# A word of the entry tile cleared behind every sixth list scatter, and 28 row steps instead of 3 ahead of expert 0's last products

## The chip, the core and the metric

One core of a Trainium2 chip runs the whole program. TensorE (PE) multiplies, VectorE (DVE), ScalarE (ACT) and GpSimd (POOL) do the elementwise work, SyncE (SP) issues most transfers; the indirect transfers, which gather and scatter rows by a list of indices, are issued by POOL. The metric is the device time of one execution in microseconds (us); lower is better.

## What is computed

Attention over 32 memory slots for 8 batches of 576 tokens and 8 heads gives a matrix x of 4608 rows by 512. A mixture of experts follows, of which the reference says:

```
noisy_logits = logits + noise_scale * noise
top2 = np.argpartition(-noisy_logits, 2, axis=1)[:, :2]
...
for e in range(E):            # 8 experts
    for k in range(2):
        mask = top2[:, k] == e
        h = np.maximum(x[mask] @ w1[e], 0.0)          # 512 -> 1024
        out[mask] += top2_w[mask, k, None] * (h @ w2[e])   # 1024 -> 512
```

Every token goes to two of eight experts, so each expert has a list of about 1150 tokens.

## The kernel before

**Routing.** The tokens are worked off in four pairs of batches, P = 0 to 3, each of 9 tiles of 128 tokens. `gate` finds the two experts of each token, builds in the tile `ent` one 16-word entry for each of a token's two choices (the first two words hold the row number and the weight, the others are zero), and sends 18 indirect scatters (L570), one for each tile and choice, which put the entries into the experts' lists in memory. Three `ent` tiles are used in turn. Scatters are declared independent of each other, except that in the first three pairs every sixth one waits for the scatter issued before it (`hold`). POOL issues the scatters, and between them the products `vb` (L341) of the attention.

**Rows of an expert.** An expert's rows, at most 1216, come in two halves of five tiles (expert 0: four groups, 0 to 3). For experts 1 to 7 `gather_sums` fetches a half in three row tiles (128, 128 and 64 rows or, in the second half, 32). For each row tile two gathers on POOL (L793) bring `gsum` and `gtile`; DVE forms sums and differences in place (L810, L811, L825, L826); ACT writes their upper half precision part and DVE the rest, in three splits: `ghalf<-gsum`, `ghalf<-gtile`, `gsplit<-gsum` (L820, L821); each split is followed by a transposing transfer on SP's queue into the tile `xt` (L822). For expert 0 `gather` does the same without sums (L757, L768, L771, L772). The gathered tiles, the splits and `xt` live in rings of two or three buffers, so a step may have to wait until an earlier transfer has read its buffer.

**Products of an expert.** `mm1` (expert 0, L935) and `mm1_sums` (experts 1 to 7, seven products of sums for each of four column blocks, L851) multiply `xt` by w1; the result is cut into `hh` and `hl` by ACT and DVE (expert 0: copy `r` L941, `hh` L942, `hl` L943). `mm2` (L965) multiplies these by w2, ACT scales the result into `y` (L977), and POOL adds it to the output by an indirect transfer (L995). Expert 0 keeps its partial results in a ring of three PSUM banks, `mp`. The weights of an expert are loaded into `stg` (L604), squared and summed on ACT for a scale (L644), and split into `wh` and `wl` (ACT L654, DVE L657).

**What sets the order.** The attention and the first three groups of expert 0 are put in order by a table of times. Behind that the code's own order counts: each engine's instructions get priorities in the order in which the code emits them, and a scheduler places them by these and by what they wait for. `all_rows` is one long generator over all halves, of which each step emits one gather or one piece of a split; `step_side` advances it, and the weights' generator, by one step between the pieces of the products. A step that must not come too early yields "wait". Ahead of the loop over halves the code runs:

```
    allr = all_rows()
    ...
    pq[1] = prep(1)
    w_load(1, 0)
    run(allr, 3)
    run(pq[1], 4)
    side += [allr, pq[1]]
```

The first 8 steps of `allr` belong to expert 0's last group (0, 3), the following ones to expert 1's first half (1, 0). Before the products of a half, `need` runs `allr` on until that half is complete.

Of the kernel before, what the change touches and what calls it, by code (L numbers as in the profile page):

```python
# [20 lines left out]
NP = B // 2  # L21
# [4 lines left out]
LW = 16  # L26
# [25 lines left out]
BURST = 6  # L52
# [9 lines left out]
def tile_attn_moe(ctx, tc, q_t, phi_t, kv, wgn, noise, w1, w2, out):  # L62
    nc = tc.nc
    V, A, G, T = nc.vector, nc.scalar, nc.gpsimd, nc.tensor
# [415 lines left out]
    scatters, reads, gated = [], [], set()  # L480
    ents_used = []

    def gate(P, j0, j1):
        nj = j1 - j0
        ns = ns_all[:, P, j0:j1]
        lg = LG[P][:, j0:j1]
        isb = ISB[P][:, j0:j1]

        def t(name):
            return gs.tile([128, NJ, E], F32, name=name)[:, 0:nj]  # L490

        def t1(name):
            return gs.tile([128, NJ], F32, name=name)[:, 0:nj]

        def wide(x):
            return x[:, :, None].to_broadcast([128, nj, E])


        u, ln, r, d = t("gu"), t("gln"), t("gr"), t("gk")
        V.tensor_tensor(lg, lg, isb[:, :, None].to_broadcast([128, nj, 16]), OP.mult)  # L500
        A.activation(u, lg[:, :, 8:16], AF.Exp)
        V.tensor_scalar(r, u, 1.0, None, op0=OP.add)
        A.activation(ln, r, AF.Ln)
        V.tensor_scalar(d, r, 1.0, None, op0=OP.subtract)
        V.scalar_tensor_tensor(r, d, 0.0, d, op0=OP.is_equal, op1=OP.add)
        V.reciprocal(r, r)
        V.tensor_tensor(r, u, r, OP.mult)
        V.tensor_tensor(r, r, ns, OP.mult)
        V.scalar_tensor_tensor(ln, d, 0.0, ln, op0=OP.is_equal, op1=OP.add)
        V.tensor_tensor(ln, ln, r, OP.mult)  # L510
        nl = t("gnl")
        V.tensor_tensor(nl, ln, lg[:, :, 0:8], OP.add)
        ms, ks = [], []
        for i in range(2):
            m = t1("gm%d" % i)
            V.tensor_reduce(m, nl, axis=AX.X, op=OP.max)
            c = t("gr")
            V.tensor_tensor(c, nl, wide(m), OP.is_lt)
            V.scalar_tensor_tensor(c, c, 8.0, iota_e[:, 0:nj], op0=OP.mult, op1=OP.add)
            ix = t1("gi")  # L520
            V.tensor_reduce(ix, c, axis=AX.X, op=OP.min)
            k = t("gk%d" % i)
            V.tensor_tensor(k, iota_e[:, 0:nj], wide(ix), OP.is_equal)
            if i == 0:
                V.scalar_tensor_tensor(nl, k, -3.0e38, nl, op0=OP.mult, op1=OP.add)
            ms.append(m)
            ks.append(k)
        mb = gs.tile([128, NJ, E], BF16, name="gmb")[:, 0:nj]
        V.tensor_tensor(mb, ks[0], ks[1], OP.add)
        yield  # L530

        mbf = mb.rearrange("p j e -> p (j e)")
        pp = ptr.tile([128, 512], F32, name="tr")
        po = pp[:, 0:nj * E]
        T.matmul(po, tri, mbf, start=True, stop=False)
        for k in range(1, nj):
            T.matmul(po[:, k * E:], ones_bf, mbf[:, 0:(nj - k) * E], start=False, stop=(k == nj - 1))
        pc = pp[:, NJ * E:(NJ + 1) * E]
        for k in range(nj):
            T.matmul(pc, ones_bf, mbf[:, k * E:(k + 1) * E], start=(k == 0), stop=(k == nj - 1))  # L540
        n = 256 * sum(x < P for x in NEED)
        if j0 == 0 and n:
            V.tensor_scalar(base[:, 0:1], base[:, 0:1], float(n), None, op0=OP.max)
        ad = t("gk")
        V.tensor_tensor(ad, eoff[:, 0:nj], base[:, None, :].to_broadcast([128, nj, E]), OP.add)
        V.tensor_tensor(ad, ad, po.rearrange("p (j e) -> p j e", e=E), OP.add)
        V.tensor_tensor(base, base, pc, OP.add)
        idx = gs.tile([128, NJ, 2], I32, name="gidx", bufs=3)
        ent = ents[len(ents_used) % 3]
        ents_used.append(0)  # L550
        G.iota(ent[:, 0:nj, :, 0].bitcast(I32), pattern=[[128, nj], [0, 2]],
               base=TRASH + P * TP + j0 * 128, channel_multiplier=1)
        ai = gs.tile([128, 2, NJ], F32, name="gai")[:, :, 0:nj]
        for k in range(2):
            tt = t(("gu", "gln")[k])
            V.tensor_tensor(tt, ad, ks[k], OP.mult)
            V.tensor_reduce(ai[:, k, :], tt, axis=AX.X, op=OP.add)
        V.tensor_copy(idx[:, 0:nj].rearrange("p j k -> p k j"), ai)
        ex, den = t1("gex"), t1("gden")
        V.tensor_tensor(ex, ms[1], ms[0], OP.subtract)  # L560
        A.activation(ex, ex, AF.Exp)
        V.tensor_scalar(den, ex, 1.0, 1e-9, op0=OP.add, op1=OP.add)
        V.reciprocal(den, den)
        V.tensor_tensor(ex, ex, isb, OP.mult)
        V.tensor_tensor(ent[:, 0:nj, 0, 1], isb, den, OP.mult)
        V.tensor_tensor(ent[:, 0:nj, 1, 1], ex, den, OP.mult)
        yield
        for j in range(nj):
            for k in range(2):
                sc = G.indirect_dma_start(  # L570
                    out=lst[:, :], out_offset=bass.IndirectOffsetOnAxis(ap=idx[:, j, k:k + 1], axis=0),
                    in_=ent[:, j, k, :], in_offset=None)
                hold = P < NP - 1 and (2 * (j0 + j) + k) % BURST == 0
                for _, o in scatters[:-1] if hold else scatters:
                    tc.declare_no_dep(sc.ins, o.ins, reason="distinct list slots")
                scatters.append((P, sc))
                for p, o in reads:
                    if p < P:
                        tc.declare_no_dep(sc.ins, o.ins, reason="slots of earlier pairs")
                if (j0 + j, k) == (NJ - 1, 1):  # L580
                    gated.add(P)
                yield
# [16 lines left out]
    def w_load(e, i):  # L599
        WS[e, i] = {}  # L600
        loaded[e, i] = ticks[0]
        for c in (3, 0, 1, 2) if e == 1 and i == 0 else (0, 2, 1, 3) if e else range(4):
            s = WS[e, i][c] = mpool.tile([128, 1024], F32, name="stg%d" % c)
            d = nc.sync.dma_start(s, (w1, w2)[i][e, c])  # L604
            if e == 0:
                after(d, "kv", BUF["w2" if i else "w1"] + c * BUF["ws"])
# [396 lines left out]
    def run(it, n=10 ** 9):  # L1003
        for _ in range(n):
            x = next(it, "end")
            if x == "end":
                return
            ticks[0] += x == "wait"
# [104 lines left out]
    def routing(P, j0, j1, end):  # L1113
        t = max(end + max(0.0, PRI["gate"]), gate_at[-1])
        g = gate(P, j0, j1)
        add(t, run, g, 1)
        t = add(t + max(0.0, PRI["g2"]), run, g, 1)
        gate_at.append(add_low(t + max(0.0, PRI["gs"]), PRI["sc%d" % P], run, g))
# [50 lines left out]
    def all_rows():  # L1169
        for k, x in enumerate(seq):  # L1170
            yield from rows_in(k, *x)
            ready.add(x)
    allr = all_rows()
# [3 lines left out]
            run(it, 1)  # L1177
    pq[1] = prep(1)
    w_load(1, 0)
    run(allr, 3)  # L1180
    run(pq[1], 4)
    side += [allr, pq[1]]
    for k, (e, g) in enumerate(seq):
# [78 lines left out]
```

## Time and profile before

| | us |
|---|---|
| median of 3 runs | 1004.69 (1001.67 to 1005.63) |
| the profiled execution | 1002.9 |
| its span, first to last instruction | 1000.9 |
| PE busy in the span | 918.5 (92%) |
| DVE, ACT, POOL busy | 616.2, 579.4, 337.2 |
| longest single wait of PE from 200 us on | 13.72 |

All times of the trace are counted from the span's start. The program's parts follow each other on PE: attention with expert 0's first groups up to about 260 us, expert 0's last group from 261.6 to 300.8, then experts 1 to 7, some 94 us each.

### The profile page before, as it was taken

To read this page: it belongs to the slowest core of one execution; us is meant where nothing else is said; L and a number is where in the kernel's file an instruction comes from. 1 tells how busy PE (TensorE), PEld (TensorE's weight loads), DVE (VectorE), ACT (ScalarE), POOL (GpSimd) and SP (SyncE) were. 2 spreads that over 40 slices of the span, in tenths; PEclk is the share of its full clock that TensorE was granted. 3 is DMA by queue.
4 is the path that set the end of the run, shared out by engine and by line. 5 is a ranking of instruction groups with operands and counts; after the bars stand their busy time and mean duration, and the time that the engine had idled before them with its cause. 6 is when DMAs were issued, how large, how long until landed. Compare 5 with 4: busy or idle time off the path is not lost.

```text
span 1000.9 us, 17556 instructions
## 1 busy us (share of the span) xinstructions
PE 918.5 (92%) x6440; PEld 540.0 (54%) x6440; DVE 616.2 (62%) x1407; ACT 579.4 (58%) x1187; POOL 337.2 (34%) x307
## 2 busy tenths in 40 slices
PE   3898996989894999999999999999999999999995
PEld 2465654655342555465555656564646564656552
DVE  1547788642662858575866776576849585957140
ACT  3577775532542756656665767576757666765241
POOL 3122654774222142414141514232333323240303
PEclk9999997999997999999999999999999999999997
DMA  9999979937687778776786869586947794775403
GB/s 319 316 308 324 352 268 344 224 83 119 121 140 98 161 120 162 149 146 99 180 151 116 132 147 179 98 163 120 204 85 148 141 213 74 158 123 82 63 1 48
DMA packets 197910, 162.01 MB, mean 162 GB/s; under 512 B 152064, under 2 KB 162496, under 8 KB 195776
## 3 DMA queue, kind: packets, MB, share of 16 engines
q1 hardware_dynamic: 178144, 120.43, 49.2%
q0 software_dynamic: 19680, 40.45, 23.9%
q8 instruction: 51, 0.84, 0.4%
q14 instruction: 35, 0.29, 0.1%
HBM read 86.77 MB, written 41.07 MB: 128 GB/s over the span
## 4 chain that ended last, share of the span: by engine, by line
PE 66%; DMA 10%; DVE 9%; ACT 4%; issue 4%; POOL 2%; SPq 2%; POOLq 0%; ACTq 0%; DVEq 0%
PE ps L965 18%; PE mp L965 15%; PE ps L851 13%; PE mp L851 7%; DMA xt<-ghalf 4%; PE pb L851 3%; PE mp L935 3%; SPq L703 2%; DMA stg<-in_w 1%; PE xp L470 1%; PE xp L355 1%; DMA phs<-in_phi_t 1%; PE tr L435 1%; PE tr L315 1%; DVE wl L657 1%
## 5 line engine op out<-in xcount | busy, mean ns | idle before, releaser
L995 POOL DMA_INDIRECT out<-y,lt x80 | 137.3, 1716 | 269.3 <-ACT y L977 239.1
L965 PEld LDWEIGHTS <-hh 128*128 128x128 f16 (+2 forms) x1504 | 122.3, 99 | 145.2 <-issue 15.9
L851 PE MATMUL ps<-xt,wh 128*128 128x320 f16 (+1 forms) x560 | 140.1, 295 | 17.6 <-DMA xt<-ghalf 15.1
L965 PE MATMUL ps<-wh,hl 128*128 128x512 f16 (+2 forms) x400 | 125.4, 380 | 0.0
L965 PE MATMUL ps<-wl,hh 128*128 128x512 f16 (+2 forms) x400 | 124.9, 380 | 0.0
L965 PE MATMUL ps<-wh,hh 128*128 128x512 f16 (+2 forms) x400 | 121.5, 380 | 0.0
L851 PEld LDWEIGHTS <-wh 128*128 128x128 f16 x896 | 87.0, 98 | 54.7 <-DMA xt<-ghalf 16.1
L965 PE MATMUL mp<-wh,hh 128*128 128x512 f16 (+2 forms) x352 | 113.0, 380 | 3.5 <-ACT hh L864 1.3
L965 PE MATMUL mp<-wl,hh 128*128 128x512 f16 (+2 forms) x352 | 113.0, 380 | 0.0
L965 PE MATMUL mp<-wh,hl 128*128 128x512 f16 (+2 forms) x352 | 112.0, 380 | 0.8 <-DVE hl L865 0.8
L965 PEld LDWEIGHTS <-hl 128*128 128x128 f16 (+2 forms) x752 | 63.1, 99 | 72.5 <-issue 6.9
L851 PE MATMUL ps<-xt,whx 128*128 128x320 f16 (+1 forms) x336 | 96.3, 292 | 0.0
L793 POOL DMA_INDIRECT gtile<-xs,lt x28 | 32.2, 1151 | 186.8 <-DVE ghalf L821 148.6
L654 ACT ACTIVATE wh<-stg,wsc 128x512 f16<-128x512 f32 x112 | 76.1, 713 | 30.8 <-DVE wsc L381 19.6
L570 POOL DMA_INDIRECT lst<-gent,gidx x72 | 72.1, 1002 | 37.0 <-issue 20.0
L657 DVE SCALAR_TENSOR_TENSOR wl<-stg,wsc,wh 128x1024 f16<-128x1024 f32 (+1 forms) x63 | 73.0, 1161 | 14.9 <-ACT wh L654 14.5
L851 PEld LDWEIGHTS <-whx 128*128 128x128 f16 x672 | 65.8, 98 | 28.0 <-issue 3.8
L644 ACT ACTIVATE wl<-stg 128x1024 bf16<-128x1024 f32 x56 | 58.6, 1047 | 28.9 <-DMA stg<-in_w 22.2
L851 PE MATMUL ps<-xt,wl 128*128 128x320 f16 (+1 forms) x280 | 73.7, 295 | 0.0
L857 ACT ACTIVATE r<-ps 128x320 f32<-128x320 f32 (+1 forms) x112 | 46.8, 421 | 39.7 <-PE ps L851 26.4
L793 POOL DMA_INDIRECT gsum<-xs,lt x42 | 48.1, 1144 | 63.1 <-DVE gsplit L821 52.8
L851 PE MATMUL mp<-xt,wh 128*128 128x320 f16 (+1 forms) x224 | 64.8, 292 | 0.9 <-DMA xt<-ghalf 0.7
(214 smaller groups left out, 1852.8 us busy)
## 6 DMA issues: line engine op xcount, KB each, us to landing
stg<-in_w SPq DMA_DIRECT2D x64, 512.0 KB
kvs<-in_kv SPq DMA_DIRECT2D x16, 1024.0 KB
out<-zt SPq DMA_DIRECT2D x38, 256.0 KB
qs<-in_q_t SPq DMA_DIRECT2D x16, 576.0 KB
xs<-xr SPq DMA_DIRECT2D x36, 256.0 KB
phs<-in_phi_t SPq DMA_DIRECT2D x16, 288.0 KB
kvs<-in_kv SPq DMA_DIRECT2D x16, 128.0 KB
xt<-ghalf SPq DMA_TRANSPOSE x88
```

Of the source, the lines that this page charges most:

```text
L315: mark["kv", u] = T.matmul(pk[h * 32:(h + 1) * 32, 0, :], es[:K, c, h * 32:(h + 1) * 32], kvs[:K, c, h, :], start=(c == 0), stop=(c == 4))
L570: sc = G.indirect_dma_start(out=lst[:, :], out_offset=bass.IndirectOffsetOnAxis(ap=idx[:, j, k:k + 1], axis=0), in_=ent[:, j, k, :], in_of ...
L644: (id if first else pace)(A.activation(wl[:, c * 1024:c * 1024 + 1024].bitcast(BF16), s[c], AF.Square, accum_out=am[:, c:c + 1]))
L654: (id if first else pace)(A.activation(h[:, o + k:o + k + 512], x[:, k:k + 512], AF.Identity, scale=sc))
L657: V.scalar_tensor_tensor(l[:, o:o + n], x, sc, h[:, o:o + n], op0=OP.mult, op1=OP.subtract)
L703: d = nc.sync.dma_start(dst, src)
L793: G.indirect_dma_start(out=x[:n], out_offset=None, in_=xs[:, :], in_offset=bass.IndirectOffsetOnAxis(ap=ix.bitcast(I32), axis=0))
L851: mark["pe"] = T.matmul(ps[:, :nh], t[w][:, o:o + 128], xt[:, 4 * k0 + 2 * n0 * lo + 2 * (a - k0) + c, :nh], start=(first and m == 0), sto ...
L857: A.activation(y[:, :nh], ps[:, :nh], AF.Identity, scale=SHC)
L935: d = mark["pe"] = mark["mm1", g] = T.matmul(ps[:, :n], ww[:, c * FF + f * 128:c * FF + (f + 1) * 128], xt[:, xo + c, :n], start=(k == 0), ...
L965: mark["pe"] = T.matmul(ps[lo:lo + x.shape[-1]], x, ws, start=start, stop=stop)
L995: d = G.indirect_dma_start(out=out[:, :], out_offset=bass.IndirectOffsetOnAxis(ap=LT[e][:n, t, 0:1].bitcast(I32), axis=0), in_=y[:n], in_o ...
```

## The change

Every sixth scatter of the first three pairs no longer waits for the one before it. Instead POOL clears the last word (which is zero already) of the entry that the sixth and the twelfth scatter of a pair read; such a write has to wait until that scatter's transfer has read the entry. These are six writes of 128 x 1 in the whole program. And `allr` is run 28 steps, not 3, before expert 1's weights and expert 0's last products are emitted.

```
-                hold = P < NP - 1 and (2 * (j0 + j) + k) % BURST == 0
-                for _, o in scatters[:-1] if hold else scatters:
+                for _, o in scatters:
                     tc.declare_no_dep(sc.ins, o.ins, reason="distinct list slots")
                 scatters.append((P, sc))
                 for p, o in reads:
                     if p < P:
                         tc.declare_no_dep(sc.ins, o.ins, reason="slots of earlier pairs")
+                if (2 * j + k) % BURST == BURST - 1 and (j, k) != (nj - 1, 1) and P < NP - 1:
+                    G.memset(ent[:, j, k, LW - 1:LW], 0.0)
...
     pq[1] = prep(1)
     w_load(1, 0)
-    run(allr, 3)
+    run(allr, 28)
     run(pq[1], 4)
```

In the changed program lines from 579 on stand one later (L820 is L821).

On DVE, in the products of expert 0's group 2 (`hh`, `hl` of 256 columns), there stood before:

```order
L771 TENSOR_TENSOR ghalf<-gtile,ghalf 128x512 x2
L942 CAST hh<-r 128x256
L943 TENSOR_TENSOR hl<-r,hh 128x256
L942 CAST hh<-r 128x256
L943 TENSOR_TENSOR hl<-r,hh 128x256
L942 CAST hh<-r 128x256
```

and now there stands:

```order
L772 TENSOR_TENSOR ghalf<-gtile,ghalf 128x512 x2
L943 CAST hh<-r 128x256
L944 TENSOR_TENSOR hl<-r,hh 128x256
L943 CAST hh<-r 128x256
L811 TENSOR_TENSOR gsum<-gtile 128x256
L944 TENSOR_TENSOR hl<-r,hh 128x256
L812 TENSOR_TENSOR gtile<-gsum,gtile 128x256
```

The two row sums of expert 1's first row tile have moved between the second `hh` and its `hl`.

On ACT, from the last square of expert 1's w1 (`wl,wam<-stg`) to the first copy `r` of expert 0's last group (448 columns), there stood before:

```order
L644 ACTIVATE wl_3546,wam<-stg_3534 128x1024
L977 ACTIVATE y<-mp,wlu 128x512
L654 ACTIVATE wh_3545<-stg_3530,wsc 128x512
L654 ACTIVATE wh_3545<-stg_3534,wsc 128x512 x2
L654 ACTIVATE wh_3545<-stg_3532,wsc 128x512
L654 ACTIVATE whx<-stg_3528,wsc 128x512 x2
L941 ACTIVATE r<-mp 128x448
```

and now there stands:

```order
L645 ACTIVATE wl_3597,wam<-stg_3540 128x1024
L821 ACTIVATE ghalf<-gsum 128x512
L821 ACTIVATE ghalf<-gtile 128x512
L978 ACTIVATE y<-mp,wlu 128x512
L821 ACTIVATE gsplit<-gsum 128x768
L655 ACTIVATE wh_3596<-stg_3536,wsc 128x512
L655 ACTIVATE wh_3596<-stg_3540,wsc 128x512 x2
L655 ACTIVATE wh_3596<-stg_3538,wsc 128x512
L655 ACTIVATE whx<-stg_3534,wsc 128x512 x2
L942 ACTIVATE r<-mp 128x448
```

The three splits of expert 1's first row tile have moved ahead of the weights' splits and of `r`; they stood among and behind them.

Also on ACT, at the end of expert 0's last group (`y` of its tiles), there stood before:

```order
L941 ACTIVATE r<-mp 128x448 x2
L977 ACTIVATE y<-mp,wlu 128x512
L977 ACTIVATE y<-ps_3820,wlu 128x512
L820 ACTIVATE ghalf<-gtile 128x512
L644 ACTIVATE wl_3810,wam<-stg_3801 128x1024
L820 ACTIVATE gsplit<-gsum 128x768
L644 ACTIVATE wl_3810,wam<-stg_3803 128x1024
L820 ACTIVATE ghalf<-gsum 64x512
L977 ACTIVATE y<-mp,wlu 128x512
L820 ACTIVATE ghalf<-gtile 64x512
```

and now there stands:

```order
L942 ACTIVATE r<-mp 128x448 x3
L821 ACTIVATE ghalf<-gsum 64x512
L821 ACTIVATE gsplit<-gsum 64x768
L978 ACTIVATE y<-mp,wlu 128x512
L821 ACTIVATE ghalf<-gtile 64x512
L978 ACTIVATE y<-ps_3848,wlu 128x512
L645 ACTIVATE wl_3826,wam<-stg_3817 128x1024
L645 ACTIVATE wl_3826,wam<-stg_3819 128x1024
L645 ACTIVATE wl_3826,wam<-stg_3821 128x1024
L645 ACTIVATE wl_3826,wam<-stg_3823 128x1024
```

The second row tile's splits are no longer in this stretch, and two of the third row tile's three (64 rows) have moved ahead of the first `y`; all four squares of expert 1's w2 stand behind it. PE's own order hardly changes there: pieces of expert 0's last `mm2` move by one column block.

## Rows read from the trace of the kernel before

**Rows 1.** the page, part 1: busy us (share of span) xinstructions by engine
```profile
PE 918.5 (92%) x6440; PEld 540.0 (54%) x6440; DVE 616.2 (62%) x1407; ACT 579.4 (58%) x1187; POOL 337.2 (34%) x307
```
**Rows 2.** waits of PE, whole span: us in total, times, longest
```profile
PE ps L851 <- DMA xt<-ghalf: 15.1, 2, 13.7
PE mp L935 <- DMA xt<-ghalf: 3.3, 1, 3.3
```
**Rows 3.** windows: length, busy us by engine, granted clock, DMA share, GB/s
```profile
262.00:301.00 39.00, 38.79 (x199) 17.93 (x197) 27.72 (x51) 19.06 (x34) 10.48 (x7) 1.00 0.66 115
301.00:314.50 13.50, 0.00 (x0) 0.00 (x0) 2.37 (x5) 1.22 (x2) 5.26 (x4) 0.63 1.25 168
314.50:318.50 4.00, 3.99 (x17) 2.32 (x18) 0.00 (x0) 2.04 (x5) 0.00 (x0) 0.54 0.47 31
318.50:600.00 281.50, 275.19 (x1805) 160.54 (x1803) 194.49 (x356) 180.11 (x333) 84.75 (x60) 1.00 0.72 139
600.00:970.00 370.00, 369.10 (x2452) 217.07 (x2450) 239.97 (x439) 228.14 (x422) 109.43 (x79) 1.00 0.69 125
```
**Rows 4.** timeline of PE: start, us, instruction, [idle before <-releaser]
```profile
254.43 0.61 PE L965 MATMUL mp<-wh,hh 128*128 128x512 f16 x2 [0.99 <-DVE hh L942]
...
267.87 0.92 PE L935 MATMUL mp<-xt,wh 128*128 128x448 f16 x4
...
314.51 0.71 PE L851 MATMUL ps<-xt,wh 128*128 128x320 f16 x2 [13.72 <-DMA xt<-ghalf]
```
**Rows 5.** the chain that ended last: start us, us, what
```profile
255.45 6.02 DMA xt<-ghalf
...
302.57 11.90 DMA xt<-ghalf
...
334.44 0.61 ACT wh L654
```
**Rows 6.** timeline of ACT
```profile
252.68 0.63 ACT L768 ACTIVATE ghalf<-gtile 128x512 f16<-128x512 f32 x1 [5.27 <-DMA xt<-ghalf]
...
258.76 2.56 ACT L654 ACTIVATE wh<-stg,wsc 128x512 f16<-128x512 f32 x4 [1.11 <-DVE wsc L381]
261.23 1.32 ACT L654 ACTIVATE whx<-stg,wsc 128x512 f16<-128x512 f32 x2
...
264.13 0.54 ACT L941 ACTIVATE r<-mp 128x448 f32<-128x448 f32 x1 [1.58 <-PE mp L935]
...
293.59 0.69 ACT L977 ACTIVATE y<-mp,wlu 128x512 f32<-128x512 f32 x1 [7.38 <-PE mp L965]
...
295.25 0.62 ACT L820 ACTIVATE ghalf<-gtile 128x512 f16<-128x512 f32 x1
```
**Rows 7.** timeline of DVE
```profile
257.69 0.29 DVE L374 TENSOR_REDUCE wsa<-pb 128x1 f32<-128x128 f32 x1 [0.42 <-PE pb L372]
...
286.93 1.15 DVE L943 TENSOR_TENSOR hl<-r,hh 128x448 f16<-128x448 f32 x2
```
**Rows 8.** timeline of POOL, the gathers of expert 1's rows
```profile
241.16 1.19 POOL L793 DMA_INDIRECT gtile<-xs,lt  x1 [0.30 <-DVE hh L942]
...
283.26 1.37 POOL L793 DMA_INDIRECT gsum<-xs,lt  x1 [7.77 <-DVE gsplit L821]
```
**Rows 9.** the page, part 6: DMA issues, KB each or median us to landing
```profile
gtile<-xs,lt POOLq DMA_INDIRECT x38, 4.6
```
**Rows 10.** windows of 2 us, columns as in rows 3
```profile
248.00:250.00 2.00, 2.00 (x12) 0.97 (x10) 0.20 (x1) 0.00 (x0) 0.00 (x0) 1.00 0.35 5
```
**Rows 11.** timeline of SP's queue: issue start, us, instruction
```profile
275.97 6.20 SPq L604 DMA_DIRECT2D stg<-in_w  x3
```
**Rows 12.** groups by line on POOL: count, busy us, mean ns, idle before
```profile
L570 POOL DMA_INDIRECT lst<-gent,gidx x72 | 72.1, 1002 | 37.0 <-issue 20.0
...
L122 POOL MEMSET hmask<- 64x1 f32 x2 | 0.2, 90 | 0.1
```
**Rows 13.** timeline of POOL, the first scatter of the last pair
```profile
197.51 1.21 POOL L570 DMA_INDIRECT lst<-gent,gidx  x1 [1.45 <-issue]
```

More of the change, by code (lines that the diff above doesn't have):

```diff
@@ L572, in gate @@
                     in_=ent[:, j, k, :], in_offset=None)
-                hold = P < NP - 1 and (2 * (j0 + j) + k) % BURST == 0
-                for _, o in scatters[:-1] if hold else scatters:
+                for _, o in scatters:
                     tc.declare_no_dep(sc.ins, o.ins, reason="distinct list slots")
@@ L579, in gate @@
                         tc.declare_no_dep(sc.ins, o.ins, reason="slots of earlier pairs")
+                if (2 * j + k) % BURST == BURST - 1 and (j, k) != (nj - 1, 1) and P < NP - 1:
+                    G.memset(ent[:, j, k, LW - 1:LW], 0.0)
                 if (j0 + j, k) == (NJ - 1, 1):
@@ L1179, in tile_attn_moe @@
     w_load(1, 0)
-    run(allr, 3)
+    run(allr, 28)
     run(pq[1], 4)
```

## Prediction

> **What bounds the kernel now.** First the busy shares by engine: PE works 918.5 of the span's 1000.9 us, and no other engine over 616.2 [rows 1]. So time is to be had where PE stands still, and only if it works without a break behind that place. The windows show that it does: 369.10 of 370 us from 600 on, 275.19 of 281.5 between 318.5 and 600, both at a granted clock of 1.00 [rows 3]. An expert's work on PE doesn't shrink or grow by this change, so what PE gains or loses around 300 us should arrive at the end nearly whole.
>
> Then PE's waits: the largest behind the attention is the one for a transposed row tile ahead of expert 1's first sum product, 15.1 us in two pieces, one of 13.7 [rows 2]. The timeline puts it at 300.79 to 314.51 [rows 4]. Around it the windows show PE full at 262 to 301 (38.79 of 39), idle to 314.5, and then 4.0 us of work at a granted clock of 0.54, about the lower of the two levels (1.2 against 2.4 GHz); from 318.5 it is 1.00 [rows 3]. In those 4.0 us PE did what takes 4.0 x 0.54 = 2.16 us at full clock: the wait costs 13.72 + 1.84 = 15.6 us in all.
>
> Last the chain that ended last, for why: the transposing transfer that frees PE is issued at 302.57 and lands at 314.47 [rows 5], 11.9 us under a DMA share of 1.25 [rows 3]. It carries a piece of the third row tile; that tile's splits came on ACT behind one of the second tile's, which ran at 295.25, itself behind a `y` that had waited 7.38 us for PE [rows 6]. So expert 1's first rows are late because their splits stand among expert 0's last products in the engines' queues, and the engines work those queues in order.
>
> **Part 1, the scatters.** Removed: a wait of every sixth scatter for the one ahead. The 72 scatters occupy POOL 72.1 us, 1002 ns each, with 20.0 us of their idle time put down to issue and none to a transfer in the group's row [rows 12]; I give the removal nothing. Added: six clearings of 128 x 1. The nearest row is a clearing of 64 x 1, 90 ns [rows 12]; with a gap of about 0.3 us, that in front of a POOL instruction in [rows 8], six are 2.4 us if all were on the path. Each must wait until its scatter has read its entry, and the next scatter stands behind it. No row shows that wait. From below it is nothing (the last two clearings fall where POOL idles 1.45 us ahead of the last pair's first scatter [rows 13]); from above, a whole landing of an indirect transfer, 4.6 us by [rows 9], six times, 28 us of POOL's, which POOL at 337.2 busy us [rows 1] can largely absorb, and of which only what delays the first gather of expert 0 would count. I take 0, with -0.5 to +2.4, because the lists are done some 45 us ahead of the place where PE waits.
>
> **Part 2, 28 steps.** Now the whole first row tile of expert 1 (both gathers, both sums, three splits, their transposes) and the second tile's first steps stand ahead of expert 1's weight splits and of expert 0's last products. Step by step:
>
> *The sums on DVE.* They stand between `hh` and `hl` of expert 0's group 2. Their gather is issued at 241.16 [rows 8]; 4.6 us [rows 9] later is 245.8, and by 248 to 250 the DMA engines move only 5 GB/s [rows 10], so 248 at the latest. DVE is held for up to some 6 us and PE, with its three banks, for an estimated 1.5. This costs nothing while PE must wait 3.3 us anyway for expert 0's last rows, which land at 261.47 [rows 2, 5]; without that cover it costs 1.5.
>
> *The splits on ACT.* The second split (`ghalf<-gtile`) needs a `ghalf` buffer that a transpose still reads, and the one landing at 261.47 [rows 5] is the one that frees it. Behind it on ACT stand `y`, `gsplit<-gsum`, the weights' copies and then `r` of expert 0's last group. Counted on: 261.5 + 0.62 (`ghalf`) + 0.69 (`y`) [rows 6] + about 0.8 (`gsplit`, half as many columns again as `ghalf`) = 263.6; then DVE's part, about 1, and the scale's chain from DVE's reduction at 257.69 to ACT's first copy at 258.76, 1.07 [rows 7, 6], make 265.7; then copies of 2.56 + 1.32 [rows 6] = 269.6. With a few tenths between engines the first `r` comes at 269.5 to 270.4 where it came at 264.13 [rows 6]. PE's third column block, at 267.87 [rows 4], needs the bank that this `r` frees 0.54 us later: it slips by 2.2 to 3.1 us, **2.7 lost**. The ends are 0, if ACT gets the buffer from an earlier transpose, and 6.2, if PE took over the whole lateness of `r`. That ACT's wait of 5.27 us at 252.68 left PE only 0.99 [rows 6, 4] speaks for a value well below the upper end.
>
> The Trainium skill bears on this ("TensorE: Matmul & The Clock Gate", section "Architectural detail: the array is 16× 32×32, not 1× 128×128"): ACT and DVE work their queues strictly first in, first out, so an instruction that waits holds all behind it. The trace agrees: the split at 295.25 follows the `y` that waited 7.38 us [rows 6]. It speaks against this change as well as for it, since moved splits now hold weights and `r`; what it would cost taken whole is the first rival.
>
> *The weights' splits and `hl` on DVE.* They begin at about 265.8, not 257.69: 8.1 us later. But some 4.8 us of row work that stood among them is done by then, so the last `hl`, 288.08 before (286.93 + 1.15 [rows 7]), ends at about 291.4, in step with PE, which ends expert 0's products at 300.8 + 2.7 = 303.5.
>
> *The third tile.* Two of its three splits (64 rows) now stand right behind the last `r`, at about 290 on ACT; DVE's part is done at 291, and its transposes go out at about 292. Landing takes between 3.3 us (an estimate, the quick end) and 11.90 [rows 5]: 295 to 304, against PE's arrival at 303.5. **The 13.72 us are gone**, or all but half a microsecond, and with them the slow clock, 1.84. Late next would be the third split, behind `y` at about 296.6 (293.59 [rows 6] and the slip): by 11.90 it lands at 306 or so and is first read some 5 us into the products, 308. And the gather at 283.26, which waited 7.77 us for a buffer [rows 8], comes earlier. Expert 1's w2, loaded at 275.97 to 282 [rows 11], comes later on SP behind more transposes, at 277 to 288 by the count of what stands ahead, but its four squares now stand together at 298 to 303, and its splits should end about 14 us earlier than the 334.44 of the chain [rows 5].
>
> **Sum.** 13.72 + 1.84 - 2.7 = 12.9 us, less 0.5 because the slip at 268 to 271 may leave some products at the lower clock: 12.4. The profiled execution took 1002.9, so 990.5; it lies 1.8 below the median of the runs shown, 1004.69, so I say **992**, with 989 to 995.5 for this case. A measurement of this kernel tells about 0.5%, 5 us, from no change.
>
> **The rivals.**
> 1. *The hold on ACT taken whole.* All 6.2 us of lateness of `r` (270.4 - 264.13) reach PE, and the break lowers the clock as the long one did, 1.84: 15.6 - 8.0 = 7.5, **997**. For it: only three banks stand between PE and ACT. Against: the 0.99 for 5.27 above. 0.18.
> 2. *All of the gain, no slip.* The `ghalf` buffer comes free early, so `r` is in time: 15.6, and the shorter second wait for a transpose (15.1 - 13.7 = 1.4 [rows 2]) with it: 17, **987**. Against: the chain shows the transpose ending at 261.47. 0.13.
> 3. *It does little.* The transposes still land late, since 11.9 us in flight came under a share of 1.25 [rows 3] and the same number of bytes must now pass beside w2's load. If the third tile's splits slip to 299, PE starts at 312 (of 314.5, with the lower clock again): 2.5 gained, **1002**. Against: at 290 it has 13 us until PE asks. 0.09.
> 4. *Slower.* w2's load stands on SP's queue behind five transposes, not two. If one of these waits for its split, the load waits too, and so the squares, the splits, and PE in expert 1's second products. The splits ended at about 334.44 [rows 5]; every microsecond later than that, plus the 12.4 won ahead of it, makes PE wait. It decides from a load at about 293, 17 us after 275.97 [rows 11]; at 305 the balance is 5 to 7 lost, **1010**. Against: the transposes ahead are those of tiles one and two, whose splits are done by about 270. 0.05.
>
> The forecast keeps 0.55. Faster by over 0.5% are the forecast, both first rivals, and a share of what is between them and the third: 0.87; within 0.5% mainly the third, 0.09; slower the fourth, 0.04. The range, from the second rival's edge to past the first, is 988 to 999: it leaves out the third, the fourth and half of the second.
>
> **What would show it.** PE's wait ahead of its first sum product, now at about 303, under 1 us, and the clock 1.00 behind it. ACT's first `r` of 448 columns at about 270, and PE's break of 2 to 3 us at 268 to 271. DVE's first sum waiting until about 246. ACT's `ghalf` of 64 rows at about 290. The four squares of w2 side by side ahead of expert 1's first product. On POOL, clearings of about 0.1 us, with no wait in front and scatters at their old pace. It is wrong if the slip at 268 is 5 us or more, if the wait at 303 has only moved to the third split or to w2's pieces, or if the clearings show waits that reach expert 0's first gather.

## The result, and the profile after

The changed kernel takes 989.91 us (median of 4 runs, 987.02 to 991.54), the kernel before 1005.16 in the same comparison (1001.67 to 1006.39): ratio 0.9851, interval 0.9816 to 0.9885. Faster, by 15.2 us of medians; 992 with 988 to 999 was forecast. The two profiled executions lie closer together, 1002.9 and 991.54, with spans of 1000.9 and 989.6: 11.3 us between the spans. What follows is read from these traces.

The page of the kernel after, part 1, beside [rows 1]:

```profile
PE 920.4 (93%) x6440; PEld 541.7 (55%) x6440; DVE 614.2 (62%) x1407; ACT 580.8 (59%) x1187; POOL 336.8 (34%) x313
```

The work is the same; the six more instructions on POOL are the clearings. The waits of PE in the changed kernel (us in total, times, longest), beside [rows 2]:

```profile
PE mp L936 <- ACT r L942: 9.8, 3, 4.0
...
PE mp L852 <- DMA xt<-ghalf: 4.1, 4, 2.3
...
PE mp L936 <- DMA xt<-ghalf: 2.5, 1, 2.5
```

The group with 13.7 us is gone. In its place waits for ACT's `r` have grown (before: 4.0 us, one wait). Where they stand, the timeline of PE shows, beside [rows 4]:

```profile
247.28 1.01 PE L936 MATMUL mp<-stg,wh 128*128 128x256 f16 x4 [2.93 <-ACT r L942]
...
262.93 0.92 PE L936 MATMUL mp<-xt,wh 128*128 128x448 f16 x4 [2.47 <-DMA xt<-ghalf]
...
272.17 0.92 PE L936 MATMUL mp<-xt,wh 128*128 128x448 f16 x4 [2.81 <-ACT r L942]
...
305.02 0.45 PE L852 MATMUL ps<-xt,wh 128*128 128x320 f16 x2
```

The first sum product of expert 1 stands at 305.02 with nothing in brackets: PE came and went on without a wait. The windows of the changed kernel (length, busy us by engine, granted clock, DMA share, GB/s), beside [rows 3]:

```profile
262.00:304.00 42.00, 38.26 (x192) 17.81 (x194) 31.54 (x58) 25.98 (x44) 16.08 (x10) 1.00 0.76 155
304.00:318.50 14.50, 14.50 (x112) 10.13 (x107) 10.39 (x25) 9.55 (x19) 5.27 (x3) 1.00 0.66 122
318.50:600.00 281.50, 277.72 (x1817) 159.61 (x1816) 192.63 (x353) 181.78 (x333) 88.72 (x65) 1.00 0.75 141
600.00:958.00 358.00, 355.35 (x2354) 209.62 (x2351) 231.34 (x420) 218.29 (x404) 100.77 (x73) 1.00 0.69 124
```

From 304 to 318.5, where PE had stood still and then run at 0.54, it works 14.50 of 14.50 us at 1.00. The price is ahead of that: 3.7 idle us between 262 and 304, of which 0.9 stand ahead of expert 0's last group and 2.81 at 272.17.

The upstream part of the program varies between executions by one or two microseconds, so the traces are compared below from one place that all have, the first product of expert 0's last group (448 columns). It stands at 262.93 above, and before at 261.61:

```profile
261.61 0.92 PE L935 MATMUL mp<-xt,wh 128*128 128x448 f16 x4 [3.31 <-DMA xt<-ghalf]
```

From there to the first sum product it was 52.90 us, and is 42.09; to the end of PE's last product (988.56 before, 977.21 after) it was 726.95, and is 714.28. That is 12.7 us, beside a forecast sum of 12.4. The spans differ by less, 11.3, because this place itself comes 1.3 us later in the changed kernel's trace.

### The profile page after: what moved, and what is told of

Read it like the earlier page. It is cut to its first block, busy times and chain, and to the rows that moved or that the text cites. A ratio compares the mean times of both kernels' runs of the same rounds, so it can differ in the third digit from the quotient of the medians.

```text
span 989.6 us, 17563 instructions
## 1 busy us (share of the span) xinstructions
PE 920.4 (93%) x6440; PEld 541.7 (55%) x6440; DVE 614.2 (62%) x1407; ACT 580.8 (59%) x1187; POOL 336.8 (34%) x313
## 4 chain that ended last, share of the span: by engine, by line
PE 70%; DVE 9%; DMA 8%; issue 5%; ACT 4%; POOL 3%; POOLq 0%; SPq 0%; ACTq 0%; DVEq 0%
PE ps L966 18%; PE mp L966 15%; PE ps L852 13%; PE mp L852 7%; DMA xt<-ghalf 4%; PE pb L852 4%; PE xp L470 3%; PE mp L936 2%; PE tr L315 2%; PE xp L355 2%; PE tr L435 1%; DMA phs<-in_phi_t 1%; DMA gtile<-xs,lt 1%; DVE wl L658 1%; DMA qs<-in_q_t 1%
## 5 line engine op out<-in xcount | busy, mean ns | idle before, releaser
L658 DVE SCALAR_TENSOR_TENSOR wl<-stg,wsc,wh 128x1024 f16<-128x1024 f32 (+1 forms) x63 | 73.2, 1161 | 10.7 <-ACT wh L655 10.2
L794 POOL DMA_INDIRECT gsum<-xs,lt x42 | 45.7, 1088 | 57.8 <-DVE gsplit L822 45.8
L852 PE MATMUL mp<-xt,whx 128*128 128x320 f16 (+1 forms) x224 | 64.8, 292 | 0.0
```

The source lines that it names most:

```text
L658: V.scalar_tensor_tensor(l[:, o:o + n], x, sc, h[:, o:o + n], op0=OP.mult, op1=OP.subtract)
L794: G.indirect_dma_start(out=x[:n], out_offset=None, in_=xs[:, :], in_offset=bass.IndirectOffsetOnAxis(ap=ix.bitcast(I32), axis=0))
L852: mark["pe"] = T.matmul(ps[:, :nh], t[w][:, o:o + 128], xt[:, 4 * k0 + 2 * n0 * lo + 2 * (a - k0) + c, :nh], start=(first and m == 0), sto ...
```

## The experiments

The first four kernels ran on one chip, beside the kernel before at 1003.12 us.

**28 steps alone**, every sixth scatter waiting as before:

```
-    run(allr, 3)
+    run(allr, 28)
```

> The 28 steps alone, every sixth scatter waiting as before, no clearing. Theory A (the steps bring all of the gain, the clearing nothing): ratio to the kernel before 0.985 as for the whole change, some 990 us; PE's first sum product near 304 us without a wait. Rival B (the trace of the change accounts for 11.3 us and the medians for 15, so the clearing brings the other 3.7): ratio 0.989, some 994 us.

Measured: 986.3 us, ratio 0.9839 (0.9805 to 0.9874). Its PE timeline:

```profile
260.86 0.92 PE L935 MATMUL mp<-xt,wh 128*128 128x448 f16 x4 [0.82 <-DMA xt<-ghalf]
...
270.10 0.92 PE L935 MATMUL mp<-xt,wh 128*128 128x448 f16 x4 [2.81 <-ACT r L941]
...
302.95 0.45 PE L851 MATMUL ps<-xt,wh 128*128 128x320 f16 x2
```

The break is 2.81 us as in the changed kernel, and from the first row to the last it is 42.09 us, the same to the hundredth. Theory A; the steps bring all of it. To PE's end it is 710.8 us from the first row, against 714.3 in the changed kernel's trace, with 5.5 us of waits of PE behind that place against 8.5: two executions of the same order can differ by 3.5 us there.

**The clearing alone**, with 3 steps:

```
-    run(allr, 28)
+    run(allr, 3)
```

> The clearing alone in place of the waiting scatters, with 3 steps as before. Theory A: ratio 1.000 (0.999 to 1.002): the first scatter of the last pair at most 1 us later, the wait of 13.7 us ahead of the first sum product still there. Rival B: ratio 0.996, some 1001 us.

Measured: 1005.83 us, ratio 1.0019 (0.9996 to 1.0043). PE's wait is still there:

```profile
313.27 0.71 PE L852 MATMUL ps<-xt,wh 128*128 128x320 f16 x2 [12.78 <-DMA xt<-ghalf]
```

Theory A again: nothing that can be told from zero, and no gain. What the median of the changed kernel shows above the traces' 11.3 to 12.7 us is no gain of the clearing; it is of the size by which executions differ.

**20 steps:**

```
-    run(allr, 28)
+    run(allr, 20)
```

> The clearing, and 20 steps instead of 28: the first row tile's splits still stand ahead of the weights' copies and of r, but the third row tile's stand behind two y again. Theory A (what counts is that the third tile's splits come ahead of the first y): the break of 2.8 us near 272 as in the changed kernel, and a wait of 3 to 8 us ahead of the first sum product comes back; 994 to 998 us, ratio 0.989 to 0.993. Rival C (the first tile's move alone does it): no wait there, ratio 0.985.

Measured: 990.8 us, ratio 0.9878 (0.9846 to 0.9910), between what the two theories expected. ACT of this kernel works the third row tile's splits (64 rows) behind both `y`, as said:

```profile
293.18 0.69 ACT L978 ACTIVATE y<-mp,wlu 128x512 f32<-128x512 f32 x1 [4.76 <-PE mp L966]
...
298.36 0.63 ACT L821 ACTIVATE ghalf<-gsum 64x512 f16<-64x512 f32 x1 [3.20 <-PE mp L966]
```

But PE hardly waits, and the break is there:

```profile
269.42 0.92 PE L936 MATMUL mp<-xt,wh 128*128 128x448 f16 x4 [2.35 <-ACT r L942]
...
302.53 0.43 PE L852 MATMUL ps<-xt,wh 128*128 128x320 f16 x2 [0.42 <-DMA xt<-ghalf]
```

The half of theory A that spoke of the third tile falls: 0.42 us, not 3 to 8. SP's queue of this kernel shows that the third tile's transposes are issued at 299.86, and the first has landed 2.7 us later, when PE starts:

```profile
299.86 2.51 SPq L823 DMA_TRANSPOSE xt<-ghalf  x2
```

In the kernel before, the one issued at 302.57 needed 11.90 us [rows 5], under a DMA share of 1.25 [rows 3]; here the share is 0.75 between 298 and 302. SP's queue of the kernel before (not among the rows above) has a pile there, second and third tile together, the second of the first pair at about 297:

```profile
286.10 12.00 SPq L822 DMA_TRANSPOSE xt<-ghalf  x2
298.79 3.69 SPq L822 DMA_TRANSPOSE xt<-gsplit  x1
302.57 3.14 SPq L822 DMA_TRANSPOSE xt<-ghalf  x2
305.80 3.71 SPq L822 DMA_TRANSPOSE xt<-gsplit  x1
```

With 20 steps the second tile's have all been issued by 291.4. So it need not be the third tile that goes ahead of `y`; it is enough that the first two go earlier. That the pile made the landing long is read from these two traces and was not tried by itself. By medians the 20 steps are 4.5 us slower than the 28 steps alone (the intervals overlap), by the traces to PE's end 5.0 (715.8 against 710.8), and PE's waits behind the first product of expert 0's last group come to 10.7 us against 5.5.

**37 steps:**

```
-    run(allr, 28)
+    run(allr, 37)
```

> The clearing, and 37 steps instead of 28: now the second row tile's splits too stand ahead of the first r of 448 columns and of the weights' copies. Theory A (splits ahead of r cost what they delay it, through three banks): PE's break ahead of the third column block near 272 grows from 2.8 to 5 us or more, no wait ahead of the first sum product; 993 to 999 us, ratio 0.988 to 0.994. Rival C (further steps are harmless): ratio 0.985.

Measured: 982.95 us, ratio 0.9806 (0.9773 to 0.9838), below the 0.9851 of the change and the 0.9839 of the 28 steps alone, with intervals that overlap. Theory A's forecast of a larger break was wrong:

```profile
270.86 0.92 PE L936 MATMUL mp<-xt,wh 128*128 128x448 f16 x4 [2.07 <-ACT r L942]
...
281.88 0.43 PE L852 MATMUL ps<-xt,wh 128*128 128x320 f16 x2
```

With two tiles ahead, the scheduler lets the first `r` go ahead of the weights' copies, so it doesn't stand behind them, and the first sum products come at 281.88, in among expert 0's last `mm2`. From expert 0's last group to PE's end it is 703.1 us, 11.2 less than in the changed kernel's trace and 7.6 less than in that of the 28 steps alone. PE's waits behind that place account for some 3 of the 11.2 (8.5 us with 28 steps, 5.5 with 37). PE's busy time accounts for more:

```profile
PE 909.3 (93%) x6440; PEld 539.7 (55%) x6440; DVE 615.8 (63%) x1407; ACT 580.3 (59%) x1187; POOL 369.8 (38%) x313
```

909.3 against 920.4 for the same 6440 matmuls; from expert 0's last group on it is 697.5 against 705.0. So the products of later experts themselves go faster. Their order on PE, compared over 1900 matmuls of the later experts, is one and the same from 3 to 34 steps, and another from 37 on. The rows of the changed kernel's PE timeline show what an order can cost. Some products use only part of the array's columns (128\*32 or 128\*64 in the rows, "narrow" below), and the order cuts them into pieces between full-width ones (128\*128):

```profile
957.41 0.38 PE L966 MATMUL mp<-wl,hh 128*128 128x512 f16 x1
957.63 0.38 PE L966 MATMUL mp<-wh,hh 128*128 128x512 f16 x1
957.94 0.40 PE L966 MATMUL ps<-wh,hh 128*32 128x512 f16 x4
958.27 0.39 PE L966 MATMUL ps<-wh,hl 128*128 128x512 f16 x1
...
960.96 0.40 PE L966 MATMUL ps<-wh,hl 128*32 128x512 f16 x3
961.28 0.39 PE L966 MATMUL ps<-wh,hh 128*128 128x512 f16 x1
...
961.82 0.40 PE L966 MATMUL ps<-wl,hh 128*32 128x512 f16 x4
962.05 0.38 PE L966 MATMUL ps<-wh,hh 128*32 128x512 f16 x1
962.36 0.39 PE L966 MATMUL ps<-wh,hl 128*128 128x512 f16 x1
```

Full-width products start 0.22 us apart. Four narrow ones side by side start within 0.01 us of each other and take the place of one, but the start ahead of the piece takes 0.31 us, not 0.22, and that behind it 0.33: each piece costs some 0.2 us for its two changes of width. From expert 0's last group on PE changes to narrow products 49 times with 28 steps and 33 times with 37, so some 3 us. The Trainium skill ("TensorEngine Tiling (Array Packing)", section "Key Properties") says that a change of the tiling mode drains TensorE; these rows agree, with about 0.1 us for each change.

A cut costs a second time. Three narrow products take as long as four (0.32 and 0.33), and a fifth takes another 0.31, so a piece whose number doesn't fill its last four loses the rest. Each piece can be counted whole, without waits: from 0.22 us after the start of the full-width product ahead of it (less where that one has fewer columns) to the start of the next full-width one. In every trace the pieces hold 696 narrow products. They take 72.3 us with 28 steps, 71.1 to 72.3 in all ten traces of up to 34 steps, and 65.6 to 66.0 in the three of 37 and 46. That is 6.4 of the 11.2 us; with the waits, under 2 us are left without a place.

The next seven runs were made on two other chips, three on one and four on the other, and on both every kernel needs some 50 us more, ahead of expert 0's last group: the kernel before took 1054.58 us on the one and 1055.06 on the other. Each ratio is to the kernel before on the same chip, and the traces are compared from expert 0's last group on.

**18 steps:**

```
-    run(allr, 28)
+    run(allr, 18)
```

> The clearing, and 18 steps: of the first row tile only one split (ghalf of gsum) stands ahead of the weights' copies on ACT; the other two stand behind the first r of 448 columns. Theory A (the break of 2.8 us on PE near 272 comes from gsplit, the scale's chain behind it and the copies, all ahead of that r): the first r comes at 266 to 267.5 and the break is under 1 us; ratio to the kernel before 0.984 to 0.988, as expert 1's first sum product still starts near 301 to 303 us. Rival F (the break comes from the copies alone or from DVE's wait for a gather): still 2 to 3 us.

Measured: ratio 0.9952 (0.9920 to 0.9984), not the 0.984 to 0.988 expected. The first `r` now stands ahead of two of the three splits on ACT:

```profile
314.17 0.67 ACT L978 ACTIVATE y<-mp,wlu 128x512 f32<-128x512 f32 x1
316.90 2.56 ACT L655 ACTIVATE wh<-stg,wsc 128x512 f16<-128x512 f32 x4 [2.06 <-DVE wsc L381]
...
320.59 0.52 ACT L942 ACTIVATE r<-mp 128x448 f32<-128x448 f32 x1
321.01 0.62 ACT L821 ACTIVATE ghalf<-gtile 128x512 f16<-128x512 f32 x1
```

It comes 5.57 us behind PE's first product (315.02), where in the changed kernel it is 271.60 - 262.93 = 8.67. And PE's break is gone, which theory A had said: the third column block starts at 321.29 without a wait, 6.27 us behind the first product, as it did before (267.87 less 261.61, 6.26) and not 9.24 as in the changed kernel. But the time is not better:

```profile
315.02 0.92 PE L936 MATMUL mp<-xt,wh 128*128 128x448 f16 x4 [2.97 <-DMA xt<-ghalf]
...
321.29 0.92 PE L936 MATMUL mp<-xt,wh 128*128 128x448 f16 x4
...
356.59 0.43 PE L852 MATMUL ps<-xt,wh 128*128 128x320 f16 x2 [2.28 <-DMA xt<-ghalf]
```

PE arrives 2.8 us sooner (39.3 us behind its first product, not 42.09) and then waits 2.28 for a transpose. The 2.81 us were no loss that could simply be had back: behind them the transposes are next in line.

**34 and 46 steps:**

```
-    run(allr, 28)
+    run(allr, 34)
```

and 46 in the same place.

> The clearing, and 34 steps: ACT's order is that of 37 steps up to the end of expert 0's last r (the second row tile's splits ahead of the weights' copies and of the first or second r), but PE's order in the later experts is that of the changed kernel, which with 37 steps was another. Theory D (what 37 steps won over 28, some 0.0045 of the ratio, lies in PE's order of the later experts, where narrow products are cut into fewer pieces): ratio 0.984 to 0.987, like 28 steps; PE from its first sum product to its end 668 to 674 us. Rival E (it is the second tile's earlier splits): ratio 0.979 to 0.982.

> The clearing, and 46 steps, the whole of expert 1's first half; PE's order in the later experts is that of 37 steps. Theory D: ratio 0.979 to 0.983, like 37 steps, some 983 us; PE ends near 964 us. Rival E (each further tile moved ahead adds or costs of its own): off by 3 us or more from 37 steps.

Measured: ratio 0.9905 (0.9870 to 0.9940) with 34 steps, 0.9865 (0.9817 to 0.9913) with 46. From expert 0's last group to PE's end it is 716.7 us with 34 and 706.4 with 46, near the 714.3 of 28 steps and the 703.1 of 37. Theory D by the traces, though with 34 steps it had expected 668 to 674 us from the first sum product to PE's end and it is 691.8: the sum products start some 17 us sooner here and PE ends no sooner. With 46 the 3.3 us to the trace of 37 would by itself have been enough for rival E; the two traces of 37 steps (703.1 above, 708.3 below) lie on either side of it. The ratios for 34 and 46 lay 0.0035 above theory D's ranges, and without 28 steps on this chip they don't tell D from E. So four went together, the changed kernel among them:

> The changed kernel itself again, beside 34, 37 and 18 steps on one chip, since the chip of the last three runs needed some 50 us more ahead of expert 0's last group: ratio 0.985, and 711 to 715 us of PE from expert 0's last group's first product to PE's last.

> 34 steps again. Theory D (37 steps win over 28 by PE's order in the later experts): within 0.003 of the ratio of 28 steps beside it. Rival E (by the second tile's earlier splits): within 0.002 of that of 37 steps.

> 37 steps again: by either theory 0.004 to 0.012 below 28 steps, since its one trace gives 703 us from expert 0's last group's first product to PE's last, against 714.

> 18 steps again. Theory A: PE's break ahead of the third column block under 1 us again, but a wait of 1 to 3 us ahead of expert 1's first sum product; ratio 0.985 to 0.989, not better than 28 steps.

| steps | median us | ratio (interval) | first product of expert 0's last group to first sum product | to PE's end |
|---|---|---|---|---|
| 18 | 1045.41 | 0.9897 (0.9840 to 0.9954) | 42.7 | 718.1 |
| 28 | 1042.77 | 0.9882 (0.9832 to 0.9932) | 43.8 | 712.9 |
| 34 | 1044.01 | 0.9875 (0.9823 to 0.9927) | 22.9 | 714.6 |
| 37 | 1037.52 | 0.9845 (0.9787 to 0.9903) | 21.3 | 708.3 |

The change gains 12.3 us here, the traces' size. 34 steps start the sum products 21 us sooner than 28, and gain nothing by it; 37 steps, with the other order of the later experts, gain 5.3 by medians and some 4.5 by the traces; the ratio is 0.0037 below that of 28, just short of the 0.004 expected. Each interval taken alone covers its neighbours. 37 lies ahead of 28 here as on the first chip (there beside the 28 steps alone), and the traces with the other order, of which each spends some 6 us less in narrow pieces, bear theory D out. In the run with 18 steps PE waits 3.29 us ahead of the first sum product, a little over the 1 to 3 expected, and the ratio is a little over its range.

## Why the prediction was right

**The wait and its clock.** It gave up 13.72 + 1.84 us. Both went: 10.81 us less from expert 0's last group to the first sum product, and a clock of 1.00 behind it. The clearing alone brings neither. Together 10.81 and 1.84 make the 12.7 us of the traces.

**The slip, 2.7.** It measured 2.81 in all three traces of 28 steps, one of them on a slower chip. The count behind it holds to about a microsecond on ACT of the changed kernel; what it left out is the 0.98 us that `gsplit` waited for DVE:

```profile
262.90 0.63 ACT L821 ACTIVATE ghalf<-gtile 128x512 f16<-128x512 f32 x1 [0.46 <-DMA xt<-ghalf]
263.44 0.67 ACT L978 ACTIVATE y<-mp,wlu 128x512 f32<-128x512 f32 x1
265.09 0.84 ACT L821 ACTIVATE gsplit<-gsum 128x768 f16<-128x768 f32 x1 [0.98 <-DVE gsum L827]
267.91 2.56 ACT L655 ACTIVATE wh<-stg,wsc 128x512 f16<-128x512 f32 x4 [1.98 <-DVE wsc L381]
...
271.60 0.52 ACT L942 ACTIVATE r<-mp 128x448 f32<-128x448 f32 x1
```

The `r` was counted at 269.5 to 270.4 from a landing at 261.47; PE's first product was 1.3 us later in this execution, and 271.60 less that is 270.3. PE took over some 2.8 of about 6 us of ACT's lateness, and not all of it, and that speaks against the first rival; that the three banks took up the rest is the prediction's reading, and no run changed their number. The break left the clock at 1.00, so the 0.5 set aside for that was not spent. With 18 steps two of the three splits went behind `r`, and the break was gone, so it is shown that the splits ahead of `r` cause it.

**The sums on DVE.** Held until 245.97, as forecast (246), and longer than 1.5 us for PE:

```profile
245.97 0.42 DVE L811 TENSOR_TENSOR gsum<-gtile 128x256 f32<-128x256 f32 x1 [5.80 <-DMA gtile<-xs,lt]
```

PE lost 2.93 us at 247.28. The cover did its work: with the 28 steps alone PE lost 3.27 there, its wait for expert 0's last rows shrank from 3.3 to 0.82, and its last group began at 260.86, no later than before. In the changed kernel's own trace it began 1.3 later; the clearing alone (261.30) doesn't delay it. The trace is late from further up: its gather on POOL at 192.56 stood at 191.28 before, ahead of all the row steps that moved. What made it late was not settled.

**The third tile.** This step had the right end and a reason that was only half right. Its splits were forecast at 290, behind the last `r`, and landings of 3.3 to 11.9 us from there. They came at 292 to 298:

```profile
292.26 0.63 ACT L821 ACTIVATE ghalf<-gsum 64x512 f16<-64x512 f32 x1 [1.47 <-PE mp L966]
...
298.04 0.62 ACT L821 ACTIVATE ghalf<-gtile 64x512 f16<-64x512 f32 x1
...
299.13 1.05 ACT L645 ACTIVATE wl<-stg 128x1024 bf16<-128x1024 f32 x1
```

With 20 steps they came at 298 to 302, behind both `y`, and it was still enough. The long landing of [rows 5] was taken as a bound for what a transpose needs, while with fewer transposes under way 2.7 us did. In the changed kernel the third tile's first transpose is issued at 293.64; at 11.9 us it would have landed at 305.5, behind PE's 305.02, so the step came out by a little because transposes were quicker than the bound.

**What costs nothing.** The clearings take 0.1 us each; the last two lie where POOL idled before, and the first scatter of the last pair follows 0.90 later, behind DVE:

```profile
197.38 0.22 POOL L580 MEMSET gent<- 128x1 f32 x2
198.50 0.97 POOL L570 DMA_INDIRECT lst<-gent,gidx  x1 [0.90 <-DVE hh L943]
```

The fourth rival (w2's load late on SP) did not come: its load begins at 278.63, within the 277 to 288 counted, its four squares stand side by side from 299.13, and PE has no wait for its splits that would show among the rows above. The third rival fell with the wait.

The sum of the terms was 12.4; the two traces give 12.7 from expert 0's last group on, and the medians 15.2 and 12.3 in two comparisons of the change, and 16.8 in that of the steps alone. That the sum and the traces agree within 0.3 us is in part luck, since traces of the same order differ by 3.5.

The second rival (no slip) was excluded by that 2.81, though the medians lie between it and the forecast.

## What to carry to other kernels

When work for the next stage stands among the last work of this one in in-order queues, count at both ends: what moving it ahead saves where the next stage begins, and what it holds up where it now stands, through how many banks. A long landing in a trace may come of a pile that goes when one of it moves; take it as an upper bound, not as the price. And when a scheduler decides the order, look past the place that was edited: a step more or less there can turn the order of everything behind it, which was here worth as much as a third of the gain.

## What the runs showed of the hardware

A change of width between matmuls costs about 0.1 us each way on PE (0.31 and 0.33 us between starts, not 0.22), and one to three narrow products of 128\*32 take as long as four. A transposing transfer of the third row tile needed 2.7 us in one trace and 11.9 in another, at DMA shares of 0.75 and 1.25; that other transfers under way are the reason was not tried. And the two chips of the last seven runs need some 50 us more for the attention and expert 0's first groups: with 28 steps expert 0's last group begins there at 314.90, not 262.93, and a wait appears ahead of it that the changed kernel's first trace does not show at this line, with no releaser that the trace can name:

```profile
PE mp L936 <- issue: 18.2, 20, 3.2
```

Between 100 and 200 us its DMA share is 0.60 and its granted clock 0.77, against 0.90 and 0.91 in the changed kernel's first trace. What lies behind it is open; no run was made for it.
